# Linear attention and a squared-ReLU layer on one core: weight sums on GpSimd, w_in behind half of the values, another planned order

## The chip, the cores and the metric

The kernel runs on one core of a Trainium2 chip. Its time is the device time of an execution in microseconds (us), start to end; of several runs the median is given. One further execution was recorded by the hardware profiler. The core's engines are TensorE (PE, matmuls; PEld is its weight load), VectorE (DVE), ScalarE (ACT), GpSimd (POOL) and SyncE (SP). Each works through its own queue in order, and they wait for each other by semaphores. SP and POOL issue most of the DMAs. [...]

## The reference

For each of 8 batches and 8 heads (sequence S = 576, head width 64), cosine-weighted linear attention; its output, with the heads side by side, is the input of a two-layer block with squared ReLU.

```
phi(x)  = [relu(x) * cos(pi/2 * pos/S), relu(x) * sin(pi/2 * pos/S)]      # 64 -> 128 features
kv      = phi(k)^T @ v          z = sum over the sequence of phi(k)
x       = (phi(q) @ kv) / (phi(q) . z + 1e-6)                             # per head
h       = x @ w_in              # x: 4608 x 512, w_in: 512 x 2048
out     = relu(h)^2 @ w_out     # w_out: 2048 x 512, float32
```

## The kernel before

All matmuls are in bf16. A batch has four full tiles of 128 rows ("main", j = 0 to 3) and a tail of 64 rows (j = 4). The steps of a batch, with the names that the prediction uses:

- loads: k, v, q (main, 1 MB each, `load_main`) and kt, vt, qt (tails, two issues each, `load_tail`). Batch 0 is loaded by SP in `prologue`, batches 1 and 2 by POOL, batches 3 to 7 by SP. Each has one buffer, so a load waits until the last batch's has been read.
- features: phi of k and q (`declare_feature`, on DVE or ACT), and v cast to bf16 (`declare_v`).
- kz: kv and z, 40 small matmuls (`declare_kz`).
- num and div: numerator and denominator, then the division on DVE (`declare_num`), which gives x. Both phi(q) and x are transposed, by PE for batches 0 and 1, by a DMA transpose on SP afterwards (`declare_qT`, `declare_xT`).
- first layer: 8 matmuls of 256 columns for two blocks of 128 of the 2048 columns and half of a batch's rows (`declare_plain`), or seven products instead of eight per 2x2 block of blocks (Strassen-Winograd, P1 to P7, `declare_seven1`, batches 3 to 7). ACT takes ReLU out of PSUM, DVE squares into gT. The four-batch tails have products of their own (`tails`).
- second layer: plain rows for batch 0 (`rows`), seven products Q1 to Q7 per pair of tiles for the others (`declare_pair`).

The seven-product form needs sums of weight blocks and of activations. Those of the weights are made once: 16 sums of 128 x 512 of w_in into w1s (`declare_w1_sums`) and 8 of 128 x 1024 of w_out into w2s (`declare_w2_sums`; sum number 3 is written over a block of w2sb). Four kinds of w2s sums, numbers 1, 2, 3 and 4, are each made in two halves, c = 0 and 1. Number 2 is number 1 subtracted from a block of w_out, and number 4 a block less number 2. The first reader of w2s is pair 0 of batch 1: Q5 reads number 1, Q6 number 2, Q7 number 3, Q4 number 4. The w1s are read from batch 3 on. The sums of activations (gs1 to gs4, xs) are made on DVE for each pair or batch.

The order of the work is not written out. Each step is declared with the engines that it may run on, a cost, what it reads and writes and, for PE, a position. A planner (`Planner`) then runs through time: it starts on each engine what can start first, picks among equals by a due time worked back from PE's positions, gives out the buffers and records the order; the kernel emits it, and each engine keeps to it. A list, SHIFTS, moves the due time or the position of single steps and may fix an engine. Costs and positions set the order alone; on the chip each instruction waits for its data.

The start is written by hand: SP loads batch 0 in the order k, kt, the first half of q, vt, v in two halves by heads, the second half of q, qt. POOL waits with w_in until a part of this has landed, by means of a copy of one element out of a loaded tile into w1sb, and then issues w_in in four quarters:

```
nc.gpsimd.tensor_copy(out=w1sb[0:1, 0, 0:1], in_=mem["vt"][0:1, 0, 0, 0:1])
for i in range(4):
    load_w1(i, 4)
```

Behind this stand on POOL the loads of batch 1 and of w_out in four parts, then those of batch 2, and the stores of batch 0. PE is meanwhile kept busy with matmuls on zeros (`fill`).

Of the kernel before, what the change touches and what calls it, by code (L numbers as in the profile page):

```python
# [10 lines left out]
ALU = mybir.AluOpType  # L11
# [7 lines left out]


SHIFTS = """
23:9.5:ACT 37:-0.5 38:1.0 44:17.5:ACT 46:-1.0 53:-0.5 62:11.5 79:-2.0 85:-2.5 89:3.0 93:11.0
108:5.5 144:9.0 152:-2.0 157:9.5:ACT 191:-5.0 194:-1.0 202:-1.5 203:-3.5:ACT 204:2.0 210:3.0
238:2.5 241:2.5 243:5.0 249:-6.0 257:-4.0 260:-2.0 261:-6.0 270:2.5 271:3.5 287:-5.0 325:-2.0
335:-0.5 340:1.5 348:8.5 354:-7.0 364:-19.0 383:1.0 390:-3.5 392:1.0 417:-4.5 487:-5.0 492:1.5
516:-7.5 517:-5.5 530:39.0 533:25.5 546:9.0 563:5.5 565:12.5 573:-8.5 575:5.0 588:13.0 593:4.5
598:-2.0 611:-4.5 617:-5.5 636:-1.5 670:7.5 677:-2.0 690:1.0 698:0.0:DVE 702:22.5 703:-19.5
704:3.5:ACT 706:-4.0 715:2.0 731:-2.5 748:5.0 781:-4.5 783:-6.0 785:-7.0 787:-2.0 790:-1.0
794:-1.5 797:1.0 799:1.0 807:11.0 813:-5.5 817:-4.0 820:-7.0 822:-5.5 836:-3.5 850:-3.5
859:-34.0 860:-15.0 870:1.0 872:-4.0 884:12.0 890:49.0 893:17.0 906:5.5 907:23.5 911:3.0 917:3.0  # L30
936:-3.0 951:-12.5 957:-1.0 958:-1.5 963:-3.5 985:7.0 990:-4.0 998:3.5 1005:-4.5 1009:5.5
1023:-10.0 1024:-8.5 1030:-10.0 1041:-26.0:ACT 1042:-10.5 1133:-13.0 1143:1.5 1155:4.0 1157:3.0
1176:-4.5 1191:4.5 1209:5.5 1247:2.5 1306:-0.5
"""


# [197 lines left out]
def kernel(  # L234
# [9 lines left out]
    nc = tc.nc  # L244
# [7 lines left out]
    J = S // P  # L252
    MAIN = J * P
    TAIL = S - MAIN
    HH = H // 2
# [167 lines left out]
            TENSOR_ADD_SAT, out=out, in0=in0, in1=in1, s0=float("inf"), s1=0.0  # L423
        )

    def sub(out, in0, in1, op=ALU.subtract):
        nc.vector.tensor_tensor(out=out, in0=in0, in1=in1, op=op)  # L427

    def mm(out, lhsT, rhs, start, stop):
        nc.tensor.matmul(  # L430
# [27 lines left out]
    def declare_load(b, nm, eng, pos=None, after=()):  # L458
        src = {"k": k, "v": v, "q": q}[nm]
        queue = nc.sync if eng == "SP" else nc.gpsimd  # L460
        for part, fn, cost, size, held in (
            (nm, load_main, 0.65 if eng == "SP" else 0.9, 3.1 if eng == "SP" else 2.7, 5.8),
            (nm + "t", load_tail, 1.3, 0.42, 6.8),
        ):
            buf = loaded[part, b] = plan.buf(part)

            def load(_, fn=fn, buf=buf):
                fn(src, nm, buf.i, b, queue)

            add((eng, cost), load, w=[buf], pos=pos, size=size, after=after, held=held if eng == "SP" else None)  # L470

    def source(nm, b, j):
        return loaded[nm if j < J else nm + "t", b]
# [56 lines left out]
    def declare_kz(b, pos, engs=("ACT",)):  # L530
        ba, bb = plan.buf("F"), plan.buf("F")
        kvz = kvzb[b] = plan.buf("kvz")
        for j in range(NS):

            def kz(_, j=j):
                kp, vx = at(kp_of(b, j)), at(vxb[b, j])
                for hh in range(HH):
                    for half in range(2):
                        h = half * HH + hh
                        if j < J:  # L540
                            lhsT, rhs = kp[:, h, :], vx[:, h, :]
                        else:
                            p0, p1 = half * TAIL, (half + 1) * TAIL
                            lhsT, rhs = kp[p0:p1, hh, :], vx[p0:p1, hh, :]
                        mm(
                            bank_pair(ba, bb)[:, half, hh * E1 : (hh + 1) * E1],
                            lhsT,
                            rhs,
                            j == 0 and hh == 0,
                            j == J and hh == HH - 1,  # L550
                        )

            add(
                ("PE", T_MM65 * (2 if j < J else 1) * HH + 0.02),
                kz,
                r=[(kp_of(b, j), j % 2, "c"), (kp_of(b, j), j % 2, "s"), vxb[b, j]],
                w=[ba, bb],
                pos=pos + 0.001 * j,
            )

        def kvz_copy(eng):
            dst = at(kvz).rearrange("p (a h) e -> p a (h e)", a=2)
            copy(eng, dst, bank_pair(ba, bb)[:, :, 0 : HH * E1])

        add({e: 0.5 if e == "ACT" else 0.6 for e in engs}, kvz_copy, r=[ba, bb], w=[kvz])

    def declare_qT(b, i):
        n = 2 if i < J // 2 else 1
        src = qp_of(b, 2 * i)
        dst = qpTb[b, i] = plan.buf("qpT" if n == 2 else "qpTt")  # L570

        def qT(_):
            s = at(src)
            s = s.rearrange("p r h f -> p (r h f)" if n == 2 else "p h f -> p (h f)")
            nc.sync.dma_start_transpose(out=at(dst), in_=s)

        keys = [(src, (2 * i + r) % 2, c) for r in range(n) for c in "cs"]
        turned["q", b, i] = add(
            ("SP", 1.95 if n == 2 else 1.2), qT, r=keys, w=[dst],
            land=0.5 if n == 2 else 0.75, held=0.2 if n == 2 else 2.2, size=2.0 if n == 2 else 0.5,  # L580
        )

    def declare_qT_pe(b, j, pos, engs):
# [21 lines left out]
    def declare_num(b, j, pos):  # L605
# [19 lines left out]
                        lhsT = t[:, hh, p0:p1]  # L625
                    mm(o, lhsT, kvz[:, half * HH + hh, :], True, True)

        add(("PE", T_MM65 * n * HH + 0.015), num, r=[qT, kvzb[b]], w=bks, pos=pos)

        def div(_):  # L630
            if n == 2:
# [18 lines left out]
    def declare_xT(b, i):  # L650
        src = x_of(b, 2 * i)
        if i < J // 2:
            dst, keys = xT_of(b, i), [(src, 0), (src, 1)]
            wkeys = [(dst, 0), (dst, 1)]
        else:
            dst, keys = xTt_of(b), [(src, 0)]
            wkeys = [(dst, b % 4)]

        def xT(_):
            if i < J // 2:  # L660
                o = at(dst).rearrange("p k (r c) -> p (k r) c", r=2)
                s = at(src).rearrange("p k r c -> p (k r c)")
            else:
                o = at(dst)[:, b % 4].rearrange("p k g c -> p (k g) c")
                o = at(dst)[:, b % 4].rearrange("p k g c -> p k (g c)")
                s = at(src).rearrange("p k c -> p (k c)")
            nc.sync.dma_start_transpose(out=o, in_=s)

        turned["x", b, i] = add(
            ("SP", 1.25), xT, r=keys, w=wkeys,  # L670
            land=1.05, held=1.6 if i < J // 2 else 4.4, size=0.95 if i < J // 2 else 0.3,
        )

    def declare_xT_pe(b, j, pos, engs):
# [103 lines left out]
    def declare_w1_sums():  # L778
        for r in range(4):
# [3 lines left out]
            for n, in0, in1, op, reads in (  # L783
# [3 lines left out]
                (3, a(0, 0), a(1, 0), ALU.subtract, [key(0), key(1)]),  # L787
            ):
                add(
                    ("DVE", 0.34), lambda _, n=n, x=in0, y=in1, op=op, s=s: sub(s(n), x, y, op),  # L790
                    r=reads, w=[("w1s", n, r)],
                )

# [2 lines left out]
    def declare_x_sums(b):  # L796
# [5 lines left out]
        for n, ops, reads in (  # L802
# [2 lines left out]
            (3, lambda: (a(1, 1), a(0, 1)), xk[1]),  # L805
            (4, lambda: (a(1, 0), t(2)), xk[0] + [(buf, 2)]),
        ):
            add(("DVE", 0.34), lambda _, n=n, ops=ops: sub(t(n), *ops()), r=reads, w=[(buf, n)] + (xk[1] if n == 3 else []))

    def declare_seven1(b, r, t):  # L810

# [11 lines left out]
        def product(name, off, acc, w, x, first, reads):  # L823
# [24 lines left out]
        product("P4", 13, Bk, lambda: w1_cols(1, 1, r), lambda: Tn(4), False, [key(1), (xs, 4)])  # L848
        add(("ACT", 0.5), lambda _: relu(block(1, 0), halves(bank(Bk))), r=[Bk], w=[(rows[1], 0)])
        add(  # L850
            ("DVE", 0.63), lambda _: add_relu(block(1, 1), halves(bank(E)), halves(at(u3))),
            r=[E, u3], w=[(rows[1], 1)],
        )
        product("P3", 14, E, lambda: w1_sum(4, r), lambda: X(1, 1), False, [("w1s", 4, r)] + xk[1])
        add(
            ("DVE", 0.63), lambda _: add_relu(block(0, 1), halves(bank(E)), halves(at(u2))),
            r=[E, u2], w=[(rows[0], 1)],
        )
        for i in range(2):
            hb = i * HBH + 2 * r  # L860
            if last:
                for j in range(2):
                    add(
                        ("DVE", 0.34),
                        lambda _, i=i, j=j, hb=hb: square(gT[:, hb : hb + 2, j * TP : (j + 1) * TP], block(i, j)),
                        r=[(rows[i], j), turn], w=[gkey(hb, j)],
                    )
# [6 lines left out]


    def st_name(b):
        return "SP" if b >= 1 else "POOL"

    def st_eng(b):
        return nc.sync if b >= 1 else nc.gpsimd  # L880

    def w2_block(i, j):
        return w2sb[:, i * HBH : (i + 1) * HBH, j * DM2 : (j + 1) * DM2]
# [4 lines left out]
    def declare_w2_sums():  # L888
        q4 = lambda i: [("w2", 2 * i), ("w2", 2 * i + 1)]
        for n, in0, in1, reads in (  # L890
# [5 lines left out]
            for c in range(2):  # L896
                h = slice(c * HBH // 2, (c + 1) * HBH // 2)
                add(
                    ("DVE", 0.6),
                    lambda _, n=n, x=in0, y=in1, h=h: sub(w2_sum(n)[:, h], x[:, h], y[:, h]),  # L900
                    r=reads, w=[("w2s", n, c)] + ([("w2", c)] if n == 3 else []),
                )
            plan.writer["w2s", n] = plan.ops[-1]
# [18 lines left out]
    def declare_pair(b, pair, t):  # L922
# [7 lines left out]
        for n, ops, op, reads in (  # L930
# [2 lines left out]
            (3, lambda: (a(0, 0), a(1, 0)), ALU.subtract, gk(0)),  # L933
            (4, lambda: (a(0, 1), at(gs[2])), ALU.subtract, gk(1) + [gs[2]]),
        ):
            add(("DVE", 0.67 if n == 1 else 0.61), lambda _, n=n, ops=ops, op=op: sub(at(gs[n]), *ops(), op), r=reads, w=[gs[n]])
        acc = lambda x: bank(x)[:, 0:DM2]
        yb = lambda i, j: at(y)[:, i, j * DM2 : (j + 1) * DM2]
        u2, u3 = (lambda: at(u)[:, 0:DM2]), (lambda: at(u)[:, DM2:DM])
# [129 lines left out]
    def prologue():  # L1069
# [17 lines left out]
            nc.vector.memset(mem[t][:, :, :, D:E1], 1.0)  # L1087
        constants()
        fill(28)
        nc.gpsimd.tensor_copy(out=w1sb[0:1, 0, 0:1], in_=mem["vt"][0:1, 0, 0, 0:1])  # L1090
        for i in range(4):
            load_w1(i, 4)

# [4 lines left out]
    given = lambda keys, t, **kw: add(("GIVEN", 0.0), lambda _: None, w=keys, pos=t, **kw)  # L1098
    L = lambda nm: loaded[nm, 0]
    for keys, t in (  # L1100
        ([L("k")], 6.25), ([L("kt")], 6.7), ([(L("q"), 0)], 8.2), ([L("vt")], 9.0), ([(L("v"), 0)], 10.75),
        ([(L("v"), 1)], 12.15), ([(L("q"), 1)], 14.2), ([L("qt")], 14.6),
    ):
        given(keys, t, lat=0.0)
    for i in range(4):
        given([("w1", i)], 11.7 + 0.01 * i, size=2.6)

    def declare_first():
        feature = lambda nm, j, c: declare_feature(nm, 0, j, c, BOTH)
# [154 lines left out]
    for s in range(8):  # L1264
        for i in range(2):
            declare_plain(1, s % 4 * 4 + 2 * i, s // 4, T1[1] + s * 2 * PROD2 + i * PROD2, s == 0)
    declare_att(2, T2[1], [T2[1] + 1.7 + 1.75 * i for i in range(NS)], BOTH, BOTH, BOTH)
    for nm in "qkv":
        declare_load(3, nm, "SP", after=[turned["q", 2, J // 2]])
    declare_w2_sums()  # L1270
    declare_pair(1, 0, T2[1])
# [70 lines left out]
```

## Time and profile before

| what | us |
|---|---|
| median of three runs | 278.17 (278.01 to 278.46) |
| the profiled execution | 276.82 |
| its span, first to last instruction | 274.8 |
| PE busy | 267.9 |
| DVE busy | 218.9 |
| ACT busy | 194.9 |
| POOL busy | 21.6 |

The span is what the trace covers; the profiled execution's own time has 2.0 us around it. The page gives, besides busy times, the span in 40 slices of 6.9 us with a digit for the busy tenths of each, the chain of waits that ended last, and groups of like instructions with their mean duration. A line of an engine's order of time has the start, the length, the queue, the line of the kernel, the operation, what it writes from what it reads, how many were merged, and in brackets the idle time before it with what ended it. PEclk was full in all slices. The sums of weights were on DVE between 22 and 61 us: 16 of 0.42 us each on w1s, 8 of 0.68 us on w2s and w2sb; in a row, the next one starts 0.34 and 0.6 us after the last.

### The profile page before, as it was taken

The page shows a single profiled execution, that of the slowest core. Times are in us where ns is not written, and L with a number is a line of the kernel's source. Part 1 is how long each engine was busy: PE and PEld are TensorE (multiplying, and loading weights), DVE is VectorE, ACT ScalarE, POOL GpSimd, SP SyncE. Part 2 cuts the span into 40 slices and gives each one's busy share as a digit, 9 for nine tenths or more (in the row PEclk, how much of TensorE's full clock was granted, in tenths as well). Part 3 has the DMA queues.
Part 4 walks back from the last instruction along what each step waited for, and adds up shares of the span by engine and source line. Part 5 has one row for each costly group of instructions (what it writes and reads, how often), then busy time and mean ns, then how long its engine had stood idle before and what let it go on. Part 6 is the DMA issues. An engine that isn't in the chain of part 4 may idle for free.

```text
span 274.8 us, 7115 instructions
## 1 busy us (share of the span) xinstructions
PE 267.9 (98%) x2845; PEld 227.6 (83%) x2845; DVE 218.9 (80%) x515; ACT 194.9 (71%) x391; POOL 21.6 (8%) x38
## 2 busy tenths in 40 slices
PE   8979999999999999999999999999999999999994
PEld 3668856789988988888888898988988888888884
DVE  1789996997694989699968999799968798279652
ACT  3876982997895598589957994699735954684522
POOL 1453544010000000000000000000000000000000
PEclk9999999999999999999999999999999999999999
DMA  7999999969979998899299955996198301200025
GB/s 217 321 205 290 296 283 365 219 218 225 361 160 186 281 334 156 224 347 221 81 164 308 259 181 102 265 338 217 35 205 170 91 2 44 95 16 2 1 79 153
DMA packets 81840, 53.01 MB, mean 193 GB/s; under 512 B 53584, under 2 KB 77648, under 8 KB 81808
## 3 DMA queue, kind: packets, MB, share of 16 engines
q1 hardware_dynamic: 75136, 40.12, 58.4%
q0 software_dynamic: 6528, 12.32, 17.1%
q8 instruction: 22, 0.36, 0.5%
q10 hardware_dynamic: 144, 0.13, 0.1%
q14 instruction: 10, 0.08, 0.1%
HBM read 36.70 MB, written 9.44 MB: 168 GB/s over the span
## 4 chain that ended last, share of the span: by engine, by line
PE 80%; DMA 8%; DVE 7%; issue 1%; SPq 1%; POOL 1%; ACT 1%; DVEq 0%
PE banks L430 79%; DMA w1sb<-in_moe_w_in_dram 4%; DMA qpT<-qp 2%; DMA vt<-in_v_dram 2%; DVE rs L422 2%; DVE gT L419 2%; DVE gs L427 2%; PE banks L591 1%; DVE x L639 1%; POOL w1sb L373 1%; SPq L366 0%; PE banks L682 0%; DVE qp L408 0%; DVE kp L408 0%; SPq L358 0%
## 5 line engine op out<-in xcount | busy, mean ns | idle before, releaser
L430 PEld LDWEIGHTS <-w1sb 128*128 128x128 bf16 x784 | 73.0, 98 | 10.4 <-DMA w1sb<-in_moe_w_in_dram 1.4
L430 PE MATMUL banks<-xT,w1sb 128*128 128x256 bf16 (+1 forms) x576 | 68.4, 267 | 1.0 <-DMA w1sb<-in_moe_w_in_dram 1.0
L430 PEld LDWEIGHTS <-gs 128*128 128x128 bf16 x512 | 49.0, 98 | 5.9 <-DVE gs L427 0.2
L416 ACT ACTIVATE rt<-banks 128x512 bf16<-128x512 f32 x64 | 37.2, 600 | 14.9 <-PE banks L430 9.3
L430 PEld LDWEIGHTS <-gT 128*128 128x128 bf16 x400 | 38.0, 98 | 9.0
L430 PE MATMUL banks<-w2sb,gT 128*128 128x256 bf16 (+1 forms) x288 | 44.2, 296 | 0.0
L430 PEld LDWEIGHTS <-w1s 128*128 128x128 bf16 x320 | 30.7, 98 | 3.7
L430 PE MATMUL banks<-w2sb,gs 128*128 128x256 bf16 x256 | 33.0, 273 | 0.0
L430 PE MATMUL banks<-w2s,gs 128*128 128x256 bf16 x256 | 32.2, 273 | 0.0
L422 DVE CUSTOM_DVE_ANT_0 rs<-banks,sums 128x512 bf16<-128x512 f32 x40 | 27.0, 684 | 4.5 <-ACT sums L847 3.1
L419 DVE TENSOR_TENSOR gT<-rs 128x1024 bf16<-128x1024 bf16 (+1 forms) x50 | 27.7, 579 | 1.8 <-ACT rs L416 1.0
L416 ACT ACTIVATE rs<-banks 128x512 bf16<-128x512 f32 x40 | 23.6, 604 | 3.1 <-PE banks L430 2.9
L430 PE MATMUL banks<-xs,w1s 128*128 128x256 bf16 x160 | 23.0, 273 | 0.0
L430 PE MATMUL banks<-xT,w1s 128*128 128x256 bf16 x160 | 22.9, 273 | 0.0
L419 DVE TENSOR_TENSOR gT<-rt 128x512 bf16<-128x512 bf16 x48 | 19.2, 418 | 4.5 <-ACT rt L416 4.3
L427 DVE TENSOR_TENSOR ysb<-banks,sums 128x256 f32<-128x256 f32 x32 | 13.4, 418 | 11.2 <-PE banks L430 7.3
L406 ACT ACTIVATE qp<-q,sin_col 128x512 bf16<-128x512 f32 x31 | 22.1, 738 | 0.1
L639 DVE TENSOR_TENSOR x<-banks,den 128x512 bf16<-128x512 f32 x30 | 20.7, 691 | 1.0
L406 ACT ACTIVATE kp<-k,sin_col 128x512 bf16<-128x512 f32 x30 | 21.2, 734 | 0.0
L427 DVE TENSOR_TENSOR gs<-gT 128x1024 bf16<-128x1024 bf16 x28 | 19.2, 686 | 1.1 <-PE banks L430 0.7
L413 ACT CAST vx<-v 128x512 bf16<-128x512 f32 x26 | 16.2, 636 | 0.9 <-DMA v<-in_v_dram 0.9
L637 DVE TENSOR_SCALAR den<-banks 128x8 f32<-128x8 f32 (+1 forms) x38 | 6.0, 159 | 12.5 <-PE banks L430 12.3
(106 smaller groups left out, 364.0 us busy)
## 6 DMA issues: line engine op xcount, KB each, us to landing
out_dram<-ysb SPq DMA_DIRECT2D x13, 512.0 KB, 3.5
k<-in_k_dram SPq DMA_DIRECT2D x6, 1024.0 KB, 6.4
v<-in_v_dram SPq DMA_DIRECT2D x5, 1024.0 KB, 7.9
q<-in_q_dram SPq DMA_DIRECT2D x5, 1024.0 KB, 9.3
w1sb<-in_moe_w_in_dram POOLq DMA_DIRECT2D x4, 512.0 KB, 10.5
q<-in_q_dram POOLq DMA_DIRECT2D x2, 1024.0 KB, 11.2
w2sb<-in_moe_w_out_dram POOLq DMA_DIRECT2D x4, 512.0 KB, 11.6
k<-in_k_dram POOLq DMA_DIRECT2D x2, 1024.0 KB, 11.3
```

What stands on the lines that cost most here:

```text
L373: nc.gpsimd.dma_start(out=w1sb[:, :, f0:f1], in_=moe_w_in[:, f0:f1].rearrange("(kb p) f -> p kb f", p=P),)
L406: nc.scalar.activation(out=dst, in_=src, func=ACTF.Relu, scale=col)
L413: (nc.scalar.copy if eng == "ACT" else nc.vector.tensor_copy)(out=out, in_=in_)
L416: nc.scalar.activation(out=out, in_=in_, func=ACTF.Relu)
L419: nc.vector.tensor_tensor(out=out, in0=in_, in1=in_, op=ALU.mult)
L422: nc.vector._custom_dve(TENSOR_ADD_SAT, out=out, in0=in0, in1=in1, s0=float("inf"), s1=0.0)
L427: nc.vector.tensor_tensor(out=out, in0=in0, in1=in1, op=op)
L430: nc.tensor.matmul(out=out, lhsT=lhsT, rhs=rhs, start=start, stop=stop, skip_group_check=True)
L591: nc.tensor.transpose(t[:, h, :], qp_at(b, j)[:, h, :], ident[:, :])
L637: nc.vector.tensor_single_scalar(out=d, in_=n4[:, :, :, D], scalar=EPS, op=ALU.add)
L639: nc.vector.tensor_tensor(out=x_at(b, j).rearrange("p (b k) (l d) -> p b k l d", b=n, l=2), in0=n4[:, :, :, 0:D].rearrange("p b (k l) d -> ...
```

## The change

- The one-element copy that holds back w_in reads the first half of the values instead of the first half of their tails.
- All sums of weights, 16 on w1s and 8 on w2s, go from DVE to POOL. `sub` takes an engine for that.
- The stores of batch 0 go from POOL to SP.
- Loads of queries on SP (batches 3 to 7) are ordered behind the issue of the tails of keys and values; for batch 3 they are declared last of the three.
- In batch 2 the cosine features of k and q may run on DVE alone, the casts of v on DVE or ACT.
- Several costs that the planner uses, the landing times that it is given for batch 0, and SHIFTS are different, and with them the whole order.

The diff, without the two SHIFTS lists and the entries that change a cost alone:

```diff
-    def sub(out, in0, in1, op=ALU.subtract):
-        nc.vector.tensor_tensor(out=out, in0=in0, in1=in1, op=op)
+    def sub(out, in0, in1, op=ALU.subtract, eng="DVE"):
+        (nc.gpsimd if eng == "POOL" else nc.vector).tensor_tensor(out=out, in0=in0, in1=in1, op=op)
...
+            load_after = [plan.writer[loaded[n, b]] for n in ("kt", "vt")] if eng == "SP" and nm == "q" and part == "q" else []
...
-            add((eng, cost), load, w=[buf], pos=pos, size=size, after=after, held=held if eng == "SP" else None)
+            add((eng, cost), load, w=[buf], pos=pos, size=size, after=list(after) + load_after, held=held if eng == "SP" else None)
...
                 add(
-                    ("DVE", 0.34), lambda _, n=n, x=in0, y=in1, op=op, s=s: sub(s(n), x, y, op),
+                    {"POOL": 1.3},
+                    lambda eng, n=n, x=in0, y=in1, op=op, s=s: sub(s(n), x, y, op, eng),
                     r=reads, w=[("w1s", n, r)],
                 )
...
     def st_name(b):
-        return "SP" if b >= 1 else "POOL"
+        return "SP" if b >= 0 else "POOL"
...
                 add(
-                    ("DVE", 0.6),
-                    lambda _, n=n, x=in0, y=in1, h=h: sub(w2_sum(n)[:, h], x[:, h], y[:, h]),
+                    {"POOL": 2.4},
+                    lambda eng, n=n, x=in0, y=in1, h=h: sub(w2_sum(n)[:, h], x[:, h], y[:, h], eng=eng),
                     r=reads, w=[("w2s", n, c)] + ([("w2", c)] if n == 3 else []),
                 )
...
-        nc.gpsimd.tensor_copy(out=w1sb[0:1, 0, 0:1], in_=mem["vt"][0:1, 0, 0, 0:1])
+        nc.gpsimd.tensor_copy(out=w1sb[0:1, 0, 0:1], in_=mem["v"][0:1, 0, 0, 0, 0:1])
...
-    declare_att(2, T2[1], [T2[1] + 1.7 + 1.75 * i for i in range(NS)], BOTH, BOTH, BOTH)
-    for nm in "qkv":
+    declare_att(2, T2[1], [T2[1] + 1.7 + 1.75 * i for i in range(NS)], DVE1, DVE1, BOTH)
+    for nm in "kvq":
         declare_load(3, nm, "SP", after=[turned["q", 2, J // 2]])
```

In the new order POOL has, behind the loads of batch 1 and w_out: five w1 sums; kt and q of batch 2; two w1 sums and both halves of w2s number 1; v, vt and k of batch 2; the first half of number 3 and the second of number 2; qt of batch 2; the second halves of numbers 4 and 3; nine w1 sums; the first half of number 2; the first half of number 4. PE's order up to the second layer of batch 0 is nearly the old one. In batch 1, pair 0, Q6 stands behind Q5, Q2 and one num, where it had stood right behind Q1 and kz.

## The prediction

> **What bounds the kernel now.** I read the page's busy row and slices first, then the stretches, then the order of time of each engine at the places that the change touches. The page:
>
> ```profile
> PE 267.9 (98%) x2845; PEld 227.6 (83%) x2845; DVE 218.9 (80%) x515; ACT 194.9 (71%) x391; POOL 21.6 (8%) x38
> ...
> PE   8979999999999999999999999999999999999994
> ...
> POOL 1453544010000000000000000000000000000000
> ```
>
> TensorE (PE) is the bound nearly everywhere; GpSimd (POOL) is almost empty and idle after the first quarter. The stretches (start and end in us, length, then busy time of each engine) say the same of the part where the weight sums run:
>
> ```profile
> 22.20:36.00 13.80, 13.80 (x124) 11.14 (x125) 13.60 (x40) 11.71 (x22) 6.58 (x9) 1.00 1.13 314
> 36.00:64.00 28.00, 28.00 (x306) 20.56 (x304) 24.62 (x62) 21.53 (x42) 6.48 (x9) 1.00 1.00 259
> 64.00:72.00 8.00, 8.00 (x106) 7.21 (x105) 4.19 (x10) 5.69 (x12) 0.00 (x0) 1.00 0.92 293
> ```
>
> VectorE (DVE) is full to 13.6 of 13.8 us at first, yet PE, the first busy figure, misses nothing: a faster DVE is worth nothing here. PE in order of time (start, length, work, wait before it):
>
> ```profile
> 19.64 1.05 PE L430 MATMUL banks<-xT,w1sb 128*128 128x256 bf16 x8 [0.86 <-DMA w1sb<-in_moe_w_in_dram]
> ...
> 22.19 1.05 PE L430 MATMUL banks<-xT,w1sb 128*128 128x256 bf16 x8 [0.16 <-DMA w1sb<-in_moe_w_in_dram]
> ...
> 67.07 0.41 PE L430 MATMUL banks<-vx,kp 128*128 128x65 bf16 x8
> ```
>
> Until 22.19 PE waits for quarters of w_in; from then it runs without a gap of note to the end. The distances between neighbouring matmuls show three later stalls only: 0.19 us at 99, 0.51 at 123, 0.36 at 143, together 1.06. That is all that a better order can win behind the start. 67.07 is the start of kz of batch 2, the point from which I count below.
>
> [...] No tensor_tensor of POOL is in this trace. [...] POOL, then DVE, in order of time:
>
> ```profile
> 28.45 0.89 POOL L358 DMA_DIRECT2D v<-in_v_dram  x1 [2.66 <-DMA q<-in_q_dram]
> 29.33 1.25 POOL L366 DMA_DIRECT2D vt<-in_v_dram  x2
> 31.23 1.52 POOL L380 DMA_DIRECT2D w2sb<-in_moe_w_out_dram  x2 [0.64 <-DMA w2sb<-in_moe_w_out_dram]
> ```
>
> ```profile
> 28.51 0.42 DVE L427 TENSOR_TENSOR w1s<-w1sb 128x512 bf16<-128x512 bf16 x1
> 28.85 0.72 DVE L408 TENSOR_SCALAR qp<-q,cos_col 128x512 bf16<-128x512 f32 x1
> 29.49 0.41 DVE L419 TENSOR_TENSOR gT<-rt 128x512 bf16<-128x512 bf16 x1
> ```
>
> While POOL issues the load of v, a feature on DVE takes 0.72 us where its group has 0.48; the two-input instructions beside it keep 0.42[...]. [...]
>
> **The change part by part.**
>
> *The gate of w_in.* POOL's one-element copy waited for vt and began at 8.64. It will wait for the first half of the values: issued at 5.74, 4.5 us to landing, so 10.24. The four issues behind it move by 1.6 us. The transfers move by less, as until about 13 the DMA engines still have values and queries to bring that w_in now shares them with: between 0 and 1.6, I take 1.0. PE's wait for the third quarter (22.19) moves with it, its order up to there being the same but for neighbours: +1.0, nothing covers it. Fill matmuls are one fewer, before any real work: nothing.
>
> *Sums off DVE.* 24 instructions go from DVE, 16 of 0.34 us (start to start) and 8 of 0.6: 10 us. Seven more of other kinds come to DVE from ScalarE (features, casts and copies at 0.3 to 0.5 us, some 3 us). Both ends lie where PE is full: worth 0. If DVE were late after this, its cover is gone; see below.
>
> *Sums onto POOL.* [...] What makes this dear is the queue. The sums stand behind the last w_out load, and that is late for a reason that stays: each load on POOL waits for an earlier transfer (w_in, q, then w_out, as above). Its issue ends at 32.75 now; with w_in later I take 33.6 (32.75 to 33.8). Then the new order has, up to the sum that is last but one, all 16 w1 sums and 7 of the 8 w2 sums, with the loads of batch 2 between them:
>
> - sums: [...] 34.7 us
> - issues, from their rows: kt 1.27, q 0.91, v 0.90, vt 1.25, k 0.90, qt 1.25 = 6.5 us
> - 33.6 + 34.7 + 6.5 = 74.8, if nothing holds POOL up.
>
> The last but one is the first half of w2s number 2, which Q6 of batch 1, pair 0, reads. PE would come to that Q6 at 67.07 + 1.30 (kz) + 3 x 0.87 (Q1, Q5, Q2) + 0.25 (one num) = 71.2. So PE waits 3.6 us at least by these prices, and PE runs in order: all behind waits as well. The last sum (w2s 4) [...] is read about 4 us later: covered.
>
> *The lock.* Between 34 and 72 DVE has 44 instructions [...] (19 squares, 14 features, 7 casts, 4 gs), 18.7 us, 0.43 each[...]. [...] I take it that in 8 of 10 cases it goes first when the sum ends: 23 x 0.8 x 0.43 = 7.9 us. Q6 then starts at 82.7, 11.5 late. Bounds: 0 held up (3.6 late), and DVE itself starved: of 44 it does 18 so, some 14 while POOL issues 6.5 us of loads, and 12 x 0.43 = 5 us are left, so 17 late, 20 with handovers.
>
> *Loads of batch 2 inside that queue.* q is issued at about 42.5 for 36.96, with 11.2 us to landing at 53.7; DVE has its first feature behind the second division of batch 1 (46.7) and waits there, a transposed x copy behind it, and so PE. k goes out at about 54 for 39.8, lands near 65, for kz at 67. These stalls lie before Q6 and come out of the same wait, as does the +1.0: PE can't pass Q6 before POOL. They are not added.
>
> *The rest.* Batch 0's two stores go from POOL to SP (0.6 us each, behind them the query transposes). On POOL they had waited 6.1 and 2.6 us for ysb, which would have blocked the sums; on SP, the transposes wait for the late q anyway. Queries behind the tails on SP: up to four tail issues (some 2.6 us) later, used last of the three; Q6's wait covers it. Costs and due times only order things. Of the 1.06 us of late stalls, I let half be won: -0.5. It could be all, or a new one of as much.
>
> Sum: 11.5 - 0.5 = +11.0. The profiled execution took 276.82 us (span 274.8 and 2.0 around), 1.35 under the median of the three runs: 287.8 there, 289.2 as a median.
>
> **Rivals.**
> - *No lock between two-input instructions* (0.25): only the queue counts. 74.8 - 71.2 - 0.5: +3.1, 281.3. For it: DVE's two-input instructions beside POOL's issues kept 0.42. Against it: [...] the 0.72.
> - *DVE starves* (0.13): [...] squares and features are late, and DVE is the bound to about 90: +17 to 20, 295 to 298. For it: DVE is already full before 36. Against it: it lost 10 us of work.
> - *POOL is in time* (0.11): the 23 sums must take no more than 71.2 - 33.6 - 6.5 = 31.1 us, held up included[...]. Then Q6 waits for nothing; if the reordering before 22 also hides the gate, the late stalls go: -1.06, 277.1. With the gate's +1.0, no change. For it: little is missing to the estimate. Against it: the lock must cost nothing too.
>
> **How the numbers follow.** The case of the sum has 0.5, and with it the forecast 289.2. The range goes from 280.5, just below the no-lock case, to 298, where DVE starves: left out are the case in time and the edges. Slower by over 0.2% (what a measurement of this kernel can tell from no change) is 0.90; the case in time is split, 0.04 same and 0.06 faster.
>
> **What would show it.** Right: w_in's copy on POOL at about 10.3; POOL sums from about 33.6 to past 78, of uneven length; PE waiting for POOL's w2s at Q6; DVE squares and features longer than 0.42 and 0.48 between 34 and 83 and not after; little PE idle behind. Wrong: PE without a gap between 60 and 85; sums of 1 us; a wait that is on k or q instead, larger than POOL's; or new stalls behind 100 us.

## The result and the profile after

| what | before | after |
|---|---|---|
| median, us | 278.16 (278.01 to 278.46, four runs) | 302.48 (302.04 to 303.10, four runs) |
| the profiled execution, us | 276.82 | 302.83 |
| its span, us | 274.8 | 301.1 |

The ratio is 1.0874 (95% interval 1.0850 to 1.0899): slower by 24.3 us, where 11.0 were forecast and 298 was the upper end of the range. The sign was right and the size was not. In this ratio and those below, executions more than 1.5% slower than the fastest of the same kernel are left out, so that a ratio need not be the quotient of two medians.

The page of the changed kernel, busy times and slices of 7.5 us:

```profile
PE 274.0 (91%) x2844; PEld 230.4 (77%) x2844; DVE 240.7 (80%) x498; ACT 191.8 (64%) x384; POOL 56.6 (19%) x60
...
PE   8879756937799899899999999999999999999995
...
DVE  2666999799996866886899799969995879558951
...
POOL 1453985899800000000000000000000000000000
PEclk9999979995999999999999999999999999999999
```

POOL took over the sums (56.6 us busy for 21.6). DVE lost 24 instructions, gained 7, and is busy for 22 us *more*. PE has holes in the same slices in which POOL works, and its granted clock fell to 7 and 5 tenths in two of them. By stretches (start and end, length, then busy time and count of PE, PEld, DVE, ACT, POOL, then the granted clock, DMA share, GB/s):

```profile
34.00:50.00 16.00, 10.79 (x74) 5.93 (x72) 15.77 (x12) 6.66 (x13) 13.91 (x12) 0.89 0.93 239
50.00:64.00 14.00, 10.63 (x120) 6.44 (x120) 11.89 (x17) 4.77 (x9) 10.39 (x9) 1.00 0.49 170
64.00:92.00 28.00, 19.48 (x201) 16.37 (x199) 26.84 (x42) 14.28 (x28) 17.81 (x13) 0.88 0.35 86
```

Read the counts: between 34 and 50 DVE is busy for 15.77 of 16 us with *twelve* instructions. An engine that looks full because it waits inside its instructions looks like an engine at work. DVE in order of time shows which ones (a merged row has the time of all of them):

```profile
33.15 6.46 DVE L426 TENSOR_TENSOR gT<-rt 128x512 bf16<-128x512 bf16 x1
...
41.64 8.21 DVE L415 TENSOR_SCALAR kp<-k,cos_col 128x512 bf16<-128x512 f32 x3
...
56.87 4.17 DVE L415 TENSOR_SCALAR kpt<-kt,cos_col 128x256 bf16<-128x256 f32 x1
...
61.99 7.15 DVE L415 TENSOR_SCALAR qp<-q,cos_col 128x512 bf16<-128x512 f32 x3
...
75.16 4.74 DVE L426 TENSOR_TENSOR gT<-rt 128x512 bf16<-128x512 bf16 x2
...
82.09 0.41 DVE L426 TENSOR_TENSOR gT<-rt 128x512 bf16<-128x512 bf16 x1
```

One square of 0.41 us lasts 6.46. POOL in order of time has the reason beside it: five sums in a row, and not one of them longer than 1.2 us:

```profile
33.72 2.29 POOL L434 TENSOR_TENSOR w1s<-w1sb 128x512 bf16<-128x512 bf16 x2
35.95 1.16 POOL L434 TENSOR_TENSOR w1s<-w1s,w1sb 128x512 bf16<-128x512 bf16 x1
37.06 1.16 POOL L434 TENSOR_TENSOR w1s<-w1sb 128x512 bf16<-128x512 bf16 x1
38.16 1.15 POOL L434 TENSOR_TENSOR w1s<-w1s,w1sb 128x512 bf16<-128x512 bf16 x1
...
77.51 4.38 POOL L434 TENSOR_TENSOR w2s<-w2sb,w2s 128x1024 bf16<-128x1024 bf16 x2
```

And PE, in order of time, waits for DVE, long before it comes to the Q6 that was to wait for POOL:

```profile
41.00 0.39 PE L690 MATMUL banks<-ident,xt 128*128 128x128 bf16 x2 [4.91 <-DVE xt L647]
41.19 1.91 PE L437 MATMUL banks<-w2sb,gT 128*128 128x512 bf16 x4
...
47.78 1.89 PE L437 MATMUL banks<-w2sb,gT 128*128 128x512 bf16 x8
...
52.43 1.22 PE L437 MATMUL banks<-vx,kp 128*128 128x65 bf16 x31 [2.73 <-DVE sums L420]
...
69.53 0.55 PE L437 MATMUL banks<-kvz,sums 128*128 128x65 bf16 x7 [5.42 <-DVE xT L420]
...
89.90 0.19 PE L437 MATMUL banks<-vx,kp 128*128 128x65 bf16 x1
```

kz of batch 2 begins at 89.90 (67.07 before), 22.8 us later, and up to there PE has as many matmuls of each shape as before. The delay is found again on PE. Its start is 1.6 later (the stream without gaps begins at 23.77 for 22.19). The six waits of over half a us ahead of kz (the three above and 0.94, 1.18, 1.02) come to 16.2, or 17.2 from matmul to matmul. The lowered clock adds some 4, an estimate: the granted clock is 0.50 from 40.57 to 43.97 and from 67.88 to 74.68, PE is busy there for 2.97 and 5.15 us, and at 41.19 four matmuls take the time of eight at 47.78. Behind the wait of 5.42 us it is the same: 16 matmuls of 256 columns take 3.44 us at 71.57, 64 take 7.18 at 82.89. Behind 89.90 there are a wait of 0.90 within kz and stalls of 3.4 in all (1.09 at 103, 0.48 and 0.98 at 123, 0.36 at 147, 0.46 at 150), where the kernel before has 1.06.

### The profile page after: what moved, and what is told of

It is laid out like the page before. It is cut to its first block, busy times and chain, and to the rows that moved or that the text cites. A ratio compares the mean times of both kernels' runs of the same rounds, so it can differ in the third digit from the quotient of the medians.

```text
span 301.1 us, 7130 instructions
## 1 busy us (share of the span) xinstructions
PE 274.0 (91%) x2844; PEld 230.4 (77%) x2844; DVE 240.7 (80%) x498; ACT 191.8 (64%) x384; POOL 56.6 (19%) x60
## 4 chain that ended last, share of the span: by engine, by line
PE 60%; DVE 14%; DMA 12%; issue 4%; ACT 4%; SPq 4%; POOL 1%; ACTq 0%; DVEq 0%
PE banks L437 60%; DMA v<-in_v_dram 4%; DMA w1sb<-in_moe_w_in_dram 3%; DVE kp L415 3%; SPq L373 3%; DMA k<-in_k_dram 3%; DVE qp L415 3%; DVE gT L426 3%; DMA vt<-in_v_dram 2%; DVE kpt L415 1%; ACT rt L423 1%; ACT qp L413 1%; DVE sums L420 1%; DVE vx L420 1%; SPq L365 1%
## 5 line engine op out<-in xcount | busy, mean ns | idle before, releaser
L437 PEld LDWEIGHTS <-w1sb 128*128 128x128 bf16 x784 | 73.8, 99 | 12.4 <-issue 2.5
L437 PE MATMUL banks<-xT,w1sb 128*128 128x256 bf16 (+1 forms) x576 | 71.3, 272 | 2.0 <-DVE xT L420 1.0
L437 PE MATMUL banks<-w2sb,gT 128*128 128x256 bf16 (+1 forms) x288 | 46.0, 300 | 0.0
L426 DVE TENSOR_TENSOR gT<-rt 128x512 bf16<-128x512 bf16 x48 | 29.6, 629 | 11.1 <-ACT rt L423 10.9
L437 PE MATMUL banks<-xT,w1s 128*128 128x256 bf16 x160 | 22.7, 273 | 0.0
L415 DVE TENSOR_SCALAR qp<-q,cos_col 128x512 bf16<-128x512 f32 x32 | 21.1, 683 | 0.6 <-DMA q<-in_q_dram 0.5
L413 ACT ACTIVATE kp<-k,sin_col 128x512 bf16<-128x512 f32 x29 | 20.5, 729 | 0.6 <-DMA k<-in_k_dram 0.5
L415 DVE TENSOR_SCALAR kp<-k,cos_col 128x512 bf16<-128x512 f32 x26 | 20.0, 787 | 0.2 <-DMA k<-in_k_dram 0.2
```

The source lines that it names most:

```text
L413: nc.scalar.activation(out=dst, in_=src, func=ACTF.Relu, scale=col)
L415: nc.vector.tensor_scalar(out=dst, in0=src, scalar1=0.0, scalar2=col, op0=ALU.max, op1=ALU.mult)
L426: nc.vector.tensor_tensor(out=out, in0=in_, in1=in_, op=ALU.mult)
L437: nc.tensor.matmul(out=out, lhsT=lhsT, rhs=rhs, start=start, stop=stop, skip_group_check=True)
```

## The experiments

Losses below are (ratio - 1) x 278.2 us, with the interval in brackets; each ratio was taken against the kernel before on the same chip.

**1. The lock by itself (bench_port).** What the prediction calls the lock was its author's supposition, which no view of before shows: a sum on GpSimd and a square, feature or cast on VectorE wait for each other. A kernel of its own: eight instructions of one kind on VectorE beside four of one kind on GpSimd, all 128x512, each sum on GpSimd written over the one before.

> A kernel of its own, without the attention and the layers (its output is zeros): eight VectorE instructions of one kind (square: two bf16 SBUF inputs; feature: fp32 SBUF to bf16 with a column; divide: PSUM and SBUF; bank: copy out of PSUM), each kind beside nothing, beside four GpSimd sums of 128x512, beside four GpSimd copies and beside four GpSimd memsets; at the end four sums alone. [...] beside sums the first square and the first feature last as long as the sums left to run, about 4 us with four sums of 1.1 in a row; divide and bank keep the time that they have alone; the sums keep 1.1 us. Rival (GpSimd slows all of SBUF, or VectorE and GpSimd take turns): the sums get longer than alone, to 1.5 us, and no VectorE instruction takes longer than about one sum.

VectorE's rows of the phases with squares, alone and then beside sums, copies and memsets on GpSimd:

```profile
4.01 3.64 DVE L55 TENSOR_TENSOR vo<-va 128x512 bf16<-128x512 bf16 x8
...
8.13 6.95 DVE L55 TENSOR_TENSOR vo<-va 128x512 bf16<-128x512 bf16 x8
...
15.57 4.78 DVE L55 TENSOR_TENSOR vo<-va 128x512 bf16<-128x512 bf16 x8
...
20.83 3.64 DVE L55 TENSOR_TENSOR vo<-va 128x512 bf16<-128x512 bf16 x8
```

Beside four sums, four squares take about 1.25 us each and the other four 0.42 (6.95 us for the eight, 3.64 alone). The four sums took 4.83 us alone and 5.25 beside the squares. Beside four copies, four of the squares took 0.71 (4.78 for the eight); beside memsets, which have no operand to read, all kept 0.42 (3.64), but eight features took 5.19 us for 4.14. Divisions and casts out of PSUM took 0.69 us beside everything. So the waiting is there, for squares and features; but here it cost VectorE 0.83 us for each of four squares and GpSimd 0.42 us in all. The single wait of about 4 us that was expected did not come; VectorE got in after every sum, as the rival had it.

**2. The sums back on VectorE (a_sums_dve).** In the changed kernel:

```
-                    {"POOL": 1.3},        # w1 sums
+                    {"DVE": 0.34},
-                    {"POOL": 2.4},        # w2 sums
+                    {"DVE": 0.6},
```

> The changed kernel with one part undone: the 24 weight sums on VectorE again at the costs of before, all else (gate, queries, stores, list of shifts) as changed. [...] nearly all of the 24 us go: 279 to 282, with the gate's 1 us or 2 left. Rival (the late loads and the new order do it): 290 or more.

282.68 us, ratio 1.0158 (1.0116 to 1.0199): +4.4. Some 20 of the 24.3 us go with the sums. The planner orders anew here, so the rest is not one edit's.

**3. Only the sums, put into the kernel before (b_sums_pool).** The reverse, with batch 0's stores on SyncE and the readers of a w2s sum waiting for both halves:

```
-                    ("DVE", 0.34), lambda _, n=n, x=in0, y=in1, op=op, s=s: sub(s(n), x, y, op),
+                    {"POOL": 1.3}, lambda eng, n=n, x=in0, y=in1, op=op, s=s: sub(s(n), x, y, op, eng),
...
-                    ("DVE", 0.6),
+                    {"POOL": 2.4},
...
-        return "SP" if b >= 1 else "POOL"
+        return "SP" if b >= 0 else "POOL"
```

> The kernel before with one part done: its 24 sums on GpSimd (costs 1.3 and 2.4, the readers of the w_out sums made to depend on both halves in the plan too), batch 0's stores on SyncE so that they do not stand behind the sums. Gate and all else as before. [...] most of the loss comes back, 293 to 305. Rival (loss of the gate, the order and the queries): under 285.

309.51 us, ratio 1.1135 (1.1061 to 1.1210): +31.6. VectorE in order of time has the same long instructions, though gate and queries are as before:

```profile
32.11 6.45 DVE L408 TENSOR_SCALAR kpt<-kt,cos_col 128x256 bf16<-128x256 f32 x1
...
55.40 12.66 DVE L408 TENSOR_SCALAR qp<-q,cos_col 128x512 bf16<-128x512 f32 x4
```

PE's waits of over half a us between 22.6 and 110 are all for VectorE (3.32, 0.81, 9.59, 1.37 and 2.46 us), none for GpSimd. The plan is made anew here too, so the 31.6 us are not the price of the sums alone; but the sums on GpSimd are enough to bring the long instructions and a loss of this size.

**4. No sums at all (a_nosums, a_nosums2).** The changed kernel in its own order with the 24 sums left out; their tiles are zeroed at the start, on VectorE (a_nosums) or some on each engine (a_nosums2, whose memsets are shown):

```
-                    lambda eng, n=n, x=in0, y=in1, op=op, s=s: sub(s(n), x, y, op, eng),
+                    lambda eng: None,
...
+        for t in w1s:
+            nc.vector.memset(t.rearrange("p k f -> p (k f)").bitcast(F32), 0.0)
+        for t in w2s:
+            nc.gpsimd.memset(t.rearrange("p k f -> p (k f)").bitcast(F32), 0.0)
```

> The changed kernel in its own order, with the 24 GpSimd sums left out; the tiles that they write are set to zero once at the start by VectorE, so what is multiplied with them is zero or the unsummed block. The loads on GpSimd stay. [...] 277 to 281, no VectorE square above 0.5 us. Rival (the order itself stalls the tensor engine): 290 or more, with the gaps of the changed kernel at 36, 64 and 81 us still there.

282.16 us, ratio 1.0150 (1.0103 to 1.0198). Seven memsets of 0.91 us stood ahead of VectorE's first features, so the second form:

> The changed kernel with the 24 weight sums left out; the tiles that they would fill are zeroed once at the start, half on VectorE and half on GpSimd, so the products that read them multiply zeros. What is left is the gate, the order of the queries behind keys and values, the stores on SyncE and the new plan. Theory that these cost what the changed kernel loses besides the sums: 279 to 281 us (gate +1.0 to +1.6, and small stalls). Rival, that everything but the sums is an improvement: 276 to 277.5 us.

280.00 us, ratio 1.0058 (1.0032 to 1.0083): +1.6 (0.9 to 2.3). This is the changed kernel without its sums, and the yardstick for the rest: the sums cost 24.3 - 1.6 = 22.7 us. The first stretch, in the same columns as above:

```profile
34.00:50.00 16.00, 16.00 (x155) 9.66 (x154) 8.71 (x24) 8.21 (x15) 6.57 (x9) 1.00 1.13 314
```

PE is full here, and DVE does 24 instructions in 8.71 us where it did 12 in 15.77.

**5. A gap after every sum (a_gap).** After experiment 1 the 6.46 us were a riddle: why does VectorE get in after every sum there, and after five of them here? There, each sum was written over the one before. The author's idea: VectorE gets its turn only in a gap between two sums.

```
+        if eng == "POOL" and last_sum:
+            nc.gpsimd.tensor_copy(out=tok, in_=last_sum.pop())       # one element of the sum before
         (nc.gpsimd if eng == "POOL" else nc.vector).tensor_tensor(out=out, in0=in0, in1=in1, op=op)
+        if eng == "POOL":
+            last_sum.append(out[0:1, out.shape[1] - 1, out.shape[2] - 1 : out.shape[2]])
```

> The changed kernel with a one-element GpSimd copy ahead of each sum, reading the last element of the sum before it. Theory that VectorE is held up for a whole run of sums without gaps: the copy makes a gap after every sum, VectorE gets one instruction in between, the long holds (6.46 us at 33 us) are gone, and the time falls to 285 to 295 us, although GpSimd has 23 copies more. Rival, the sums cost what they cost because of the lock at each one: 301 to 306 us, the squares as long as before in sum. Second rival, that it was GpSimd's own queue: slower than 302.5, since the queue gets longer.

306.65 us, ratio 1.1019 (1.0978 to 1.1060): +28.3. The first half of the theory held: with gaps, every long wait of VectorE ends with a sum. VectorE in order of time, to be read against the 6.46 and the 8.21 above:

```profile
33.82 2.15 DVE L416 TENSOR_SCALAR kpt<-kt,cos_col 128x256 bf16<-128x256 f32 x1
...
37.85 4.17 DVE L416 TENSOR_SCALAR kp<-k,cos_col 128x512 bf16<-128x512 f32 x3
```

The second half fell: the time went up, and kz of batch 2 began at 91.35. That is the time of the second rival, a longer queue on GpSimd; but up to kz no wait of PE is for GpSimd, whose last sum ends at 82.23 (81.89 in the changed kernel). Compared as in experiment 6, VectorE even waits less than in the changed kernel, 24.6 us for 30.0. So the sum of its waits is not all: PE waited 3.43 us shortly before kz (at 83.45, for ScalarE), and the 48 matmuls of 256 columns behind that wait took 8.05 us, where 64 of them took 7.18 in the changed kernel. Over the whole span the granted clock was 0.972 for 0.981. The lowered clock may account for some 3 of the 4 us, by an estimate that was not tested: at the rate of the 64, the 48 would have taken 5.4 us.

**6. The sums' time as what counts (a_w1only, a_w2only, a_memsets).** The theory for the size: what counts is the time for which GpSimd has sums under way, called the hold here. In the changed kernel its 24 sums, from 33.72 to 81.9, take 36.0 us. VectorE's instructions stand in the same order in the changed kernel and in a_nosums2, so that each can be compared with itself. Twelve of them, from the square at 33.15 to a feature at 80.57, last 30.0 us longer in all, and no other by more than 0.1. (Counted from 33.72 on, without that first square, it is 23.6, close to the 23 of the first expectation below.) So VectorE waited inside its instructions for five sixths of the hold. The same stretch of PE's work up to kz of batch 2, in the changed kernel and then in a_nosums2, in the columns of the stretches above:

```profile
33.15:89.90 56.75, 40.56 (x368) 28.37 (x367) 53.78 (x66) 24.71 (x46) 42.96 (x34) 0.91 0.56 153
32.33:67.85 35.52, 35.52 (x368) 25.94 (x367) 25.99 (x71) 26.48 (x49) 7.36 (x10) 1.00 0.95 256
```

For the same 368 matmuls VectorE is full in the one and has slack in the other. Three tests, all in the changed kernel's order. Half the hold, once with the 16 short sums and once with the 8 long ones (the others left out, their tiles zeroed):

> The changed kernel, in its own order, with only the 16 sums of w_in (18.4 us of GpSimd) computed; the 8 sums of w_out are left out and their tiles zeroed once at the start. [...] All 24 sums [...] made VectorE wait 23 us and cost 22.5 us of time (302.5 less 280.0 without any sum), so half of them make it wait 11 to 12 us, of which the slack that VectorE has without sums (5.5 us of the 34 before kz of batch 2) takes up to half: 285 to 292 us. Rival of the forecast, the end of GpSimd's own queue: without 17 us of sums it is through by about 65 us and no Q6 waits: 280 to 281 us.

> The same with only the 8 sums of w_out (17 us of GpSimd) computed and the 16 of w_in left out. [...] nearly the same hold, so nearly the same time, 285 to 292 us, although each hold is twice as long. Rival, that it is the long holds that hurt: near the 302 of the changed kernel, and a_w1only near 280.

a_w1only: 293.84 us, ratio 1.0546 (1.0476 to 1.0615), +15.2. a_w2only: 291.86, ratio 1.0511 (1.0459 to 1.0563), +14.2. Less the 1.6 of a_nosums2 that is 13.6 for 18.9 us of hold and 12.6 for 16.9: 0.72 and 0.75 us lost per us held, alike for short and long sums (the losses are known to some 2 us either way). All sums: 22.7 for 36.0, or 0.63. The two halves together give 26.2, a little more than the whole. So it is the time of the hold that counts, whether short or long sums make it up. In their traces VectorE waited 16.3 and 15.5 us. The expectation that its slack would take up to half was too kind: over four fifths of the waiting came out as time.

The third keeps GpSimd nearly as busy and its queue as long, without an operand to read: two memsets in the place of each sum.

```
-                    lambda eng, n=n, x=in0, y=in1, op=op, s=s: sub(s(n), x, y, op, eng),
+                    lambda eng, n=n, s=s: [nc.gpsimd.memset(s(n), 0.0) for _ in range(2)],
```

> The changed kernel, in its own order, with each sum replaced by two GpSimd memsets of the same tile (128x512 twice for a w_in sum, 128x1024 twice for a w_out sum, each pair about as long as the sum): the sums are left out, GpSimd is as busy, its queue as long and who waits for it the same, but nothing of SBUF is read. In the measurement of its own, memsets on GpSimd left VectorE's squares at 0.42 us and stretched only the features, from 0.48 to 0.70. [...] squares are free, 16 features and casts take some 0.2 to 0.5 us longer, within VectorE's slack: 280 to 285 us. Rival, GpSimd's queue or the dependencies on it: 295 to 302 us, as with the sums.

282.99 us, ratio 1.0180 (1.0124 to 1.0236): +5.0, 3.4 over a_nosums2. GpSimd, then VectorE, in order of time:

```profile
33.22 6.08 POOL L799 MEMSET w1s<- 128x512 bf16 x10
...
60.84 10.48 POOL L799 MEMSET w1s<- 128x512 bf16 x18
```

```profile
33.86 0.41 DVE L426 TENSOR_TENSOR gT<-rt 128x512 bf16<-128x512 bf16 x1
...
35.98 2.29 DVE L415 TENSOR_SCALAR kp<-k,cos_col 128x512 bf16<-128x512 f32 x3
```

GpSimd is busy with memsets for 34.2 us (36.0 with the sums), the loads of batch 2 still stand between them, and every reader of the tiles still waits for it. Squares keep 0.41, features are stretched (the three of the last row take 2.29 us for 1.27 in a_nosums2), VectorE's waiting falls from 30.0 to 8.1 us, and 85% of the loss is gone. So it is neither GpSimd's queue, late loads included, nor the dependencies on it. It is what GpSimd does beside VectorE: sums of two tensors stretched squares (to 6.46 us in the changed kernel, to 1.25 in experiment 1), memsets left them at 0.41 and 0.42.

**7. Who waits through a whole run (bench2, bench3).** These take up the riddle of experiment 5, by kernels of their own.

> A kernel of its own (it computes nothing of the reference, its output is zeros). VectorE issues eight 128x512 squares, then eight 128x512 features, beside four 128x512 two-input sums on GpSimd, once with the sums free (four destination tiles, nothing to wait for) and once with a one-element GpSimd copy ahead of each sum that reads the sum before it, so that the GpSimd engine has a gap between them. [...] beside free sums the first square or feature lasts about 4.6 us (four sums of 1.15) and the others 0.42 and 0.48; beside sums with gaps four of them last about 1.2 to 1.4 us each. Rival, [...] 1.25 us each in both, four times over, and the free sums start 1.3 to 1.6 us apart and not 1.15.

The free sums gave VectorE a turn after each, just like those with gaps: squares of 1.37 us beside free sums and 1.37 to 1.51 beside gaps. The rival held, and a missing gap is not the cause.

> A kernel of its own (it computes nothing of the reference, its output is zeros): five free 128x512 sums on GpSimd beside six 128x512 squares on VectorE, in six phases. 1: sums of plain tiles, VectorE arrives in the middle of the first (behind a copy from PSUM). 2: the same with the operands of the kernel's w_in sums (2x256 columns of a wide tile). 3: those operands, both begin together. 4 and 5: a DMA issue on GpSimd ahead of the sums, VectorE arrives during it, with wide and with plain operands. 6: a DMA issue and the copy from PSUM. Theory that an instruction of VectorE which is already waiting when GpSimd starts its first sum loses every turn: a first square of 5 to 6.5 us in phases 4, 5 and 6 and squares of 1.2 to 1.4 us in 1 to 3. Rival, the operands decide: long in 2, 3, 4 and 6, short in 1 and 5. Second rival, the arrival in the middle decides: long in 1, 2 and 6.

Phase 1 gave nothing: GpSimd was late and its sums ran alone. In phases 2 and 3 (the kernel's operands, VectorE at work before or from the middle of the first sum) a square took 0.92 to 1.37 us. In 4 to 6, where VectorE's square begins while GpSimd issues a DMA with the sums right behind it, that square lasted 6.30, 6.29 and 6.02 us: through all five sums, with either operands. Phases 3 and 4, VectorE (six squares to a row), then GpSimd:

```profile
30.55 6.86 DVE L60 TENSOR_TENSOR vs<-va 128x512 bf16<-128x512 bf16 x6
...
37.90 7.97 DVE L60 TENSOR_TENSOR vs<-va 128x512 bf16<-128x512 bf16 x6
```

```profile
30.65 6.48 POOL L78 TENSOR_TENSOR gs<-wide 128x512 bf16<-128x512 bf16 x5
...
37.97 0.68 POOL L82 DMA_DIRECT2D wide<-in_moe_w_out_dram  x1
38.68 5.57 POOL L78 TENSOR_TENSOR gs<-wide 128x512 bf16<-128x512 bf16 x5
```

Where the two take turns, the sums start 1.29 us apart (6.48 for five); where VectorE came in during the issue, they start 1.11 us apart (5.57), as they do alone in bench2 (4.46 for four), and it gets no turn. The square of 33.15 in the changed kernel began during the issue of w_out (32.21 to 33.73). Not all long waits there began so, and why the order of arrival matters in this way stays open.

**8. The other parts (b_gate_v, b_gate_kt, b_kvq).** In the kernel before, w_in's gate alone:

```
-        nc.gpsimd.tensor_copy(out=w1sb[0:1, 0, 0:1], in_=mem["vt"][0:1, 0, 0, 0:1])
+        nc.gpsimd.tensor_copy(out=w1sb[0:1, 0, 0:1], in_=mem["v"][0:1, 0, 0, 0, 0:1])     # b_gate_kt: mem["kt"][0:1, 0, 0, 0:1]
```

> The kernel before with one edit: w_in's gate reads the first half of the values and no longer their tail. Theory that the gate puts off the third quarter of w_in and with it TensorE's start: copy at 10.2 to 11.0 us for 8.64, start of the unbroken stream 1.0 to 1.6 us later than 22.19, time +1.0 to +1.6 us (279.2 to 279.8). Rival, the DMA engines are freed for values and queries and the two cancel: within 0.4 us of the kernel before.

278.42 us, ratio 1.0001 (0.9977 to 1.0024): between -0.6 and +0.7. In its profile the copy is at 11.03 and the stream begins 0.9 later (23.08), but the runs don't show it as a loss.

> The kernel before with one edit: w_in's gate reads the tail of the keys, which lands before that of the values. If the start of TensorE's unbroken stream is bound by w_in's arrival: copy at about 6.7 to 7.5 us for 8.64, stream up to 1 us earlier, 277.2 to 278 us. Rival, values and queries then share the DMA engines with w_in and come later by as much: 278 to 279.5 us.

280.97 us, ratio 1.0102 (1.0056 to 1.0149): +2.8, above both expectations. The copy came at 6.35, and PE then waited for VectorE's first division instead, 1.35 us at 16.5. The earlier gate is worse, the later one no different.

```
-    for nm in "qkv":
+    for nm in "kvq":
         declare_load(3, nm, "SP", after=[turned["q", 2, J // 2]])
...
-            add(..., after=after, ...)
+            add(..., after=list(after) + load_after, ...)     # queries of SP wait for the issue of kt and vt
```

> The kernel before with one part of the change: on SyncE's queue, the queries of a batch are loaded behind the tails of its keys and values. Theory that the remaining loss without sums is a matter of the new plan's order and not of this: within 0.7 us of the kernel before. Rival, late queries: 279 to 280 us, with stalls of TensorE behind 95 us of 0.5 to 1.5 us.

284.61 us, ratio 1.0238 (1.0199 to 1.0276): +6.6, outside both expectations. Its profile has many small waits between 80 and 195 us, for results of VectorE and ScalarE (0.90, 0.89, 0.58 us and so on), hardly one for a load. Two things changed here: the queries are later, and the planner orders everything anew with a list of shifts meant for another order. The run can't tell them apart. That the changed kernel, with the same queries and a list of its own, is only 1.6 us slower without its sums, speaks for the list.

No version came out faster than the kernel before.

## Why the prediction was right and wrong

- **Gate.** Forecast: copy at 10.24, start +1.0. The copy came at 11.02, the stream 1.6 later in the trace of the changed kernel; alone it cost between -0.6 and +0.7 in the runs. The step was read rightly, its worth in time was overrated.
- **Sums off DVE: worth 0.** Right: a_nosums2 has none at all and is 1.6 us slower than before, not faster.
- **Price and place of the sums.** The place was right: first sum at 33.72 for 33.6. The 34.7 us that the prediction sets for the first 23 sums was its author's estimate, which no view of before shows; the trace of the changed kernel has 33.8 (1.15 for the 128x512 sum at 38.16, 4.20 for the two 128x1024 sums at 44.96), and 36.0 for all 24.
- **The lock: this step failed.** The waiting itself is in the traces: in experiment 1 squares took 1.25 us beside sums for 0.42 alone, and casts out of PSUM kept their 0.69; in the changed kernel two casts of v took 2.42 us at 72.83 for 0.75 at 52.30. What failed is how I charged it. I took VectorE to go first in 8 of 10 cases and put the cost on POOL: 23 x 0.8 x 0.43 = 7.9 us, to be seen as one wait at Q6. In fact POOL was hardly held up (seven of the sums took 1.32 to 1.34 for 1.15), its last sum ended at 81.9, and Q6 at 95.14 did not wait for it. VectorE was held up instead, for 30.0 us, and PE waited for VectorE at six places ahead of Q6. My bound for a starved VectorE (17 to 20 late) had the right place but counted only VectorE's own leftover work (12 x 0.43 = 5 us), not the time for which it stands still. So the signs "uneven sums" (but for those seven) and "PE waits at Q6" did not come; "squares and features longer between 34 and 83 only" did.
- **A better sum.** Where the sums and VectorE's squares, features and casts wait for each other, their times add, whichever goes first, and Q6 needs what both do. The first sum at 33.7, the 33.8 us of the 23 sums in the trace, and the 18.7 us of the 44 VectorE instructions that the prediction counts between 34 and 72 make 86.2 for a Q6 due at 71.2, so 15 late by this estimate, where I had 11.5. It is no strict floor: in bench3 a sum and a square in turn took 1.29 us, less than 1.11 and 0.34 (start to start) one after the other. And it is still short of what came, kz 22.8 late. The sums mostly went first, and VectorE's other work (PSUM copies, divisions) stood in its queue behind the instruction that waited.
- **Rivals.** No lock (0.25) and POOL in time (0.11) fell. *DVE starves* had 0.13 and was the case, at 295 to 298 for 302.5. Against it I had said that VectorE lost 10 us of work; but it lost 10 us of work and got 30 of waiting.
- **Clock.** No step had it. TensorE's granted clock was 0.89 and 0.88 in the stretches with the long gaps (34 to 50 and 64 to 92). It was 0.50 in two parts of them, from 40.57 to 43.97 and from 67.88 to 74.68, each of which began in a wait of PE for VectorE (of 4.91 and 5.42 us). Behind the first the 512-column matmuls stand 0.43 us apart for 0.22; in the stretch from 50 to 64, with a wait of 2.73, the clock stayed at 1.00. That came to some 4 us on PE, half of the 8.1 us for which it was busy at 0.50. How much of it lay on the path was not separated, since PE was waiting for VectorE much of that time anyway.
- **The rest.** Half of the late stalls was to be won (-0.5). Instead they came to 3.4 us in the profile, for 1.06 before; a_nosums2 has the like without any sum (0.59 and 0.98 at 99, 0.45 and 0.56 at 123 to 126), so they come with the new order.

## What to carry to other kernels

Before moving elementwise work from VectorE to GpSimd, add GpSimd's whole time to that of VectorE's instructions that wait beside it (in these runs squares, features and casts beside sums, but not what reads PSUM), from the start of the first moved instruction to the next due time: if this sum passes the due time by much, expect one of the two to be late, however idle GpSimd was; who goes first decides which. Here the sum passed it by 15 us, and VectorE was late: 10 us of work taken off it came back as 30 us of waiting in it, and with it waited all that stood behind in its queue. In a profile this shows as an engine that is full with few instructions: look at counts and at the mean of a group, not at the busy share alone.

## What the runs showed of the hardware

- A square on VectorE that began while GpSimd issued a DMA with sums queued behind it waited through all five (6.29 us in bench3, 6.46 in the changed kernel), and the sums were not slowed (1.11 us apart). A wait of this kind stands inside the instruction's own time, so that VectorE counts as busy. Where VectorE was at work before the first sum, the two took turns (sums 1.29 us apart, squares of 1.37 in bench3).
- Beside GpSimd's memsets two-input squares kept 0.41 us, and eight features took 5.19 us for 4.14 alone (bench_port). Its copies and sums stretched both: eight squares took 4.78 and 6.95 us for 3.64, eight features 5.04 and 7.21. VectorE's divisions and casts out of PSUM kept 0.69 us beside all three.
